# A scan and a two-layer product: the second layer as seven half-block products, and casts and transposing DMAs in strict turns

## The chip, the cores and the metric

One core of one Trainium2 chip. The metric is device time in microseconds (us) of one execution; lower is better. A time is about 2 us longer than the span of the same execution in the trace.

## The reference

```python
# x, f_logit: (4, 6144, 256); lower_bound: (256,); w1, w2: (256, 1024); w_out: (1024, 256)
f = lower_bound + (1 - lower_bound) * sigmoid(f_logit)
h = zeros((B, D))
for t in range(S):                       # a recurrence along the 6144 steps
    h = f[:, t] * h + (1 - f[:, t]) * x[:, t]
    y[:, t] = h
y = y.reshape(24576, 256)
out = np.maximum(y @ w1, y @ w2) @ w_out
```

Both kernels use max(a, b) = a + relu(b - a). So the first layer is `relu(y @ (w2 - w1))`, 1024 wide, and the second layer adds `that @ w_out` to `y @ (w1 @ w_out)`; both kernels fold the factor (1 - lower_bound) into the weights.

## The kernel before

Tokens come in blocks of 512. Two blocks make a chunk of 1024 tokens, which the recurrence needs with features on the partitions. So each chunk of each input is cast from fp32 to bf16 by a DMA from DRAM into a scratch buffer in DRAM (issued on GpSimd, "POOL"), and transposed by a DMA from there into SBUF (issued on the sync engine, "SP"). Chunks 4 to 25, 22 of them, go that way; "cast" and "transpose" below mean these DMAs.

The parts that matter here, abridged:

```python
NSCR = 2                                  # two scratch buffers per tensor
def fetch(c):                             # casts of chunk c
    for s in range(2):                    # f, then x
        scr = scratch[s][uses[s] % NSCR]; uses[s] += 1
        nc.gpsimd.dma_start(out=scr..., in_=src...)
def cross(c):                             # transposes of chunk c
    for s in range(2):
        dst = inpool.tile([P, KC, CH], BF16, name=("fT", "xT")[s])
        nc.sync.dma_start_transpose(out=dst[:, :, 0:nt], in_=held[c, s][0:nt, :])
# ... cut: gate() is a sigmoid on ScalarE; scan_steps() is decay, drive and scan on VectorE
def first_layer(j, fc):                   # 2 matmuls of 512 columns, 1 relu
    ...
def second_layer(j, slot):                # 5 matmuls of 256 columns
    ...   # left = y or relu(..) of 128 tokens (weights of the array), right = w13 or w_out
for j in range(2, NBLK + 1):
    ahead("cross", cross, j + LEAD_CROSS)     # 3 blocks ahead
    ahead("fetch", fetch, j + LEAD_FETCH)     # 7 blocks ahead
    for fc in range(FC):                      # 8 slots
        first_layer(j, fc); second_layer(j - 1, fc)   # + gate, scans of block j + 1
```

A cast waits only until the transpose that read its own scratch buffer has landed.

Of the kernel before, what the change touches and what calls it, by code (L numbers as in the profile page):

```python
# [18 lines left out]
def kernel(  # L19
# [18 lines left out]
    CH = 1024  # L38
    assert S % CH == 0

# [15 lines left out]
    def by_xbar(c, s):  # L56
        return c >= 4
# [6 lines left out]
    natpool = ctx.enter_context(tc.tile_pool(name="nat", bufs=6))  # L64
    inpool = ctx.enter_context(tc.tile_pool(name="inp", bufs=5))
    midpool = ctx.enter_context(tc.tile_pool(name="mid", bufs=2))
    ypool = ctx.enter_context(tc.tile_pool(name="ypool", bufs=4))
    rpool = ctx.enter_context(tc.tile_pool(name="rpool", bufs=2 * FC + 4))
    opool = ctx.enter_context(tc.tile_pool(name="opool", bufs=4))
    ps_t = ctx.enter_context(  # L70
        tc.tile_pool(name="ps_t", bufs=2, space=bass.MemoryType.PSUM)
    )
    ps_d = ctx.enter_context(
        tc.tile_pool(name="ps_d", bufs=3, space=bass.MemoryType.PSUM)
    )
    ps_o = ctx.enter_context(
        tc.tile_pool(name="ps_o", bufs=3, space=bass.MemoryType.PSUM)
    )

    NSCR = 2  # L80
    scratch = [
        [dram.tile([CH, D], BF16, name=f"scr{s}_{q}") for q in range(NSCR)]
        for s in range(2)
    ]
    uses = [0, 0]
# [5 lines left out]
    def fetch(c):  # L91
        b, t0, nt, _ = chunks[c]
        for s in range(2):
            src = srcs[s][b, t0 : t0 + nt, :]
            if by_xbar(c, s):
                scr = scratch[s][uses[s] % NSCR]
                uses[s] += 1
                nc.gpsimd.dma_start(  # L98
                    out=scr[0:nt, :].rearrange("(p i) d -> p (i d)", p=P),
                    in_=src.rearrange("(p i) d -> p (i d)", p=P),  # L100
                )
                held[c, s] = scr
            else:
                nat = natpool.tile([P, CH // P, D], BF16, name=("fn", "xn")[s])
                nc.gpsimd.dma_start(
                    out=nat[:, 0 : nt // P, :].rearrange(
                        "p (k i) d -> p k (i d)", i=TB // P
                    ),
                    in_=src.rearrange(
                        "(k p i) d -> p k (i d)", p=P, i=TB // P  # L110
                    ),
                )
                held[c, s] = nat
# [3 lines left out]
    def fetch_first(k):  # L117
        nt = TB // 2
        for s in range(2):
            raw = const.tile([P, nt // P, D], FP32, name=f"raw{k}{s}")  # L120
            nc.sync.dma_start(  # L121
                out=raw[:],
                in_=srcs[s][0, k * nt : (k + 1) * nt, :].rearrange(
                    "(p i) d -> p i d", p=P
                ),
            )
            raws[k, s] = raw

    def first_bf16(k, s, copy):
        raw = raws[k, s]  # L130
        nat = const.tile([P, raw.shape[1], D], BF16, name=f"nat{k}{s}")
        copy(out=nat[:], in_=raw[:])
        raws[k, s] = nat

    def first_turn(k):
        nt = TB // 2
        for s in range(2):
            dst = ps_t.tile([P, KC, nt // P, P], BF16, name="tT")
# [9 lines left out]
    def cross(c):  # L148
        nt = chunks[c][2]
        for s in range(2):  # L150
            if by_xbar(c, s):
                dst = inpool.tile([P, KC, CH], BF16, name=("fT", "xT")[s])
                nc.sync.dma_start_transpose(  # L153
                    out=dst[:, :, 0:nt], in_=held[c, s][0:nt, :]
                )
                held[c, s] = dst

    def turn_steps(j):
        b, t0, nb, c, o = blocks[j]
        steps = []  # L160
        for s in range(2):
            if by_xbar(c, s):
                turned[j, s] = held[c, s][:, :, o : o + nb]
                continue
            dst = ps_t.tile([P, KC, TB], BF16, name="tT")
            ns = nb // P
            turned[j, s] = dst[:, :, 0:nb].rearrange("p k (i m) -> p k m i", i=ns)
            for q in range(ns):
                for h in range(KC):
                    steps.append(  # L170
                        (
                            dst[:, h, q * P : (q + 1) * P],
                            held[c, s][:, o // P + q, h * P : (h + 1) * P],
                        )
                    )
# [7 lines left out]

    us = {}

    def gate(j):
        nb = blocks[j][2]
        u = midpool.tile([P, KC, TB], BF16, name="u")
        fT = turned[j, 0]
        nc.scalar.activation(  # L190
            out=like(u[:, :, 0:nb], fT), in_=fT, func=AF.Sigmoid, scale=-1.0
        )
        us[j] = u
# [6 lines left out]
    def scan_steps(j):  # L200
        b, t0, nb, c, o = blocks[j]
        u = us[j]
        ff = midpool.tile([P, KC, TB], BF16, name="ff")
        v = midpool.tile([P, KC, TB], BF16, name="v")
        y = ypool.tile([P, KC, TB], BF16, name="y")
        ys[j] = y

        def decay(h):
            nc.vector.tensor_scalar(  # L209
                out=ff[:, h, 0:nb],  # L210
                in0=u[:, h, 0:nb],
                scalar1=nom[:, h : h + 1],
                scalar2=1.0,
                op0=ALU.mult,
                op1=ALU.add,
            )

        def drive():
            xT = turned[j, 1]
            nc.vector.tensor_tensor(  # L220
                out=like(v[:, :, 0:nb], xT),
                in0=like(u[:, :, 0:nb], xT),
                in1=xT,
                op=ALU.mult,
            )

        def scan(h):
            if t0 == 0:
                init = 0.0
            else:  # L230
                pn = blocks[j - 1][2]
                init = ys[j - 1][:, h, pn - 1 : pn]
            nc.vector.tensor_tensor_scan(  # L233
                out=y[:, h, 0:nb],
                data0=ff[:, h, 0:nb],
                data1=v[:, h, 0:nb],
                initial=init,
                op0=ALU.mult,
                op1=ALU.add,
            )  # L240

        return [
            lambda: decay(0),
            lambda: decay(1),
            drive,
            lambda: scan(0),
            lambda: scan(1),
        ]

    first = {}  # L250

    def first_recurrence(k):
        nt = TB // 2
        cols = slice(k * nt, (k + 1) * nt)
        if k == 0:
            for t in ("u", "ff", "v"):
                first[t] = midpool.tile([P, KC, TB], BF16, name=t)
            ys[0] = ypool.tile([P, KC, TB], BF16, name="y")
        u, ff, v, y = (*(first[t] for t in ("u", "ff", "v")), ys[0])
        fT, xT = raws[k, 0], raws[k, 1]  # L260
        nc.scalar.activation(
            out=like(u[:, :, cols], fT), in_=fT, func=AF.Sigmoid, scale=-1.0
        )
        for h in range(KC):
# [7 lines left out]
            )  # L272
        nc.vector.tensor_tensor(
            out=like(v[:, :, cols], xT), in0=like(u[:, :, cols], xT), in1=xT,
            op=ALU.mult,
        )
        for h in range(KC):
# [13 lines left out]

    ident_f = const.tile([P, P], FP32)
# [8 lines left out]
    wdf = wpool.tile([P, KC, DFF], FP32)  # L301
    wd = wpool.tile([P, KC, DFF], BF16)
    w1T = wpool.tile([P, FC, D], BF16)
    w13 = wpool.tile([P, KC, D], BF16)
    NG = 2
    NQ = FC // NG
    w1n = [wpool.tile([P, KC, NQ * P], FP32, name=f"w1n{g}") for g in range(NG)]
    w2n = [wpool.tile([P, KC, NQ * P], FP32, name=f"w2n{g}") for g in range(NG)]

    def half(w, g):  # L310
        return w[g][:].rearrange("p kc (m q) -> p kc q m", q=NQ)

    def fcs(w, kc, g):
        return w[:, kc, g * NQ * P : (g + 1) * NQ * P].rearrange(
            "p (q m) -> p q m", q=NQ
        )
# [12 lines left out]
    def make_wd(fc, n):  # L329
        g, r = divmod(fc, NQ)  # L330
        qs = slice(r, r + n)
        cols = slice(fc * P, (fc + n) * P)
        nc.vector.tensor_tensor(  # L333
            out=wdf[:, :, cols].rearrange("p kc (q m) -> p kc q m", q=n),
# [4 lines left out]
        for kc in range(KC):  # L339
            if g == 0:  # L340
                nc.scalar.mul(wd[:, kc, cols], wdf[:, kc, cols], om[:, kc : kc + 1])  # L341
            else:
                nc.vector.tensor_scalar_mul(
                    out=wd[:, kc, cols], in0=wdf[:, kc, cols], scalar1=om[:, kc : kc + 1]
                )

    def turn_w1(k):
        g, r = divmod(k, NQ // 2)
        pt = ps_o.tile([P, KC, 2, P], FP32, name="psO")
# [11 lines left out]
    def make_w13():  # L361
        for kc in range(KC):
            psw = ps_o.tile([P, 2, D], FP32, name="psO")
# [9 lines left out]

    rts = {}

    def first_layer(j, fc):
        nb = blocks[j][2]
        y = ys[j]
        dT = ps_d.tile([P, TB], FP32, name="dT")
        for kc in range(KC):  # L380
            nc.tensor.matmul(  # L381
                dT[:, 0:nb],
                lhsT=wd[:, kc, fc * P : (fc + 1) * P],
                rhs=y[:, kc, 0:nb],
# [3 lines left out]
        rt = rpool.tile([P, TB], BF16, name="rt")  # L388
        nc.scalar.activation(out=rt[:, 0:nb], in_=dT[:, 0:nb], func=AF.Relu)  # L389
        rts[j, fc] = rt  # L390
# [3 lines left out]
    def second_layer(j, slot):  # L394
        b, t0, nb, c, o = blocks[j]
        ns = nb // P
# [3 lines left out]
        for k in range(slot * total // FC, (slot + 1) * total // FC):  # L400
            i, s = divmod(k, n)
            g, r = divmod(i, 2)
            if s == 0 and (r == 0 or j == NBLK - 1):
                acc["ps"] = ps_o.tile([P, 2, D], FP32, name="psO")
# [3 lines left out]
            left = y[:, s, i:nb:ns] if s < KC else rts[j, s - KC][:, i:nb:ns]  # L408
            right = w13[:, s, :] if s < KC else wob[:, s - KC, :]
# [8 lines left out]
            if j == NBLK - 1 and s == n - 1:  # L418
# [3 lines left out]
                r0 = b * S + t0  # L422
                (nc.sync if r else nc.scalar).dma_start(
# [148 lines left out]
```

## Time and profile before

| kernel before | time, us |
|---|---|
| first three runs | 438.17, 401.23, 438.83 |
| with the run beside the changed kernel | median 419.7, 400.81 to 438.83 |

There are two kinds of runs: fast ones near 401 us and slow ones. The profile that the prediction had is of a slow one, span 428.3 us.

From the page of that profile: busy time by engine, and the chain of work that ended last (shares of the span). PE is TensorE, PEld its weight loads, DVE VectorE, ACT ScalarE, POOL GpSimd, SP the sync engine; a q after a name marks that engine's queue of issues and waits.

```profile
PE 392.8 (92%) x2744; PEld 296.8 (69%) x2792; DVE 248.7 (58%) x359; ACT 268.5 (63%) x447; POOL 26.4 (6%) x58
...
PE 46%; DMA 34%; SPq 15%; ACT 3%; DVE 1%; issue 1%; ACTq 0%
```

TensorE (PE) is busy 92% of the time, yet half of the chain is DMA and the sync queue. The timeline of the sync engine in the same profile (start in us, duration in us, what) shows why:

```profile
200.80 7.09 SPq L153 DMA_TRANSPOSE fT<-scr_0_90  x1
207.99 5.61 SPq L153 DMA_TRANSPOSE xT<-scr_0_92  x1
213.69 1.03 SPq L433 DMA_DIRECT2D out_dram<-osb  x2
214.82 9.81 SPq L153 DMA_TRANSPOSE fT<-scr_1_91  x1
224.73 9.85 SPq L153 DMA_TRANSPOSE xT<-scr_1_93  x1
234.67 1.01 SPq L433 DMA_DIRECT2D out_dram<-osb  x2
235.78 10.23 SPq L153 DMA_TRANSPOSE fT<-scr_0_90  x1
```

One chunk took 14.0 us (200.8 to 214.8), the next 21.0. The timeline of TensorE, one slot in steady state, gives the other pace:

```profile
204.67 0.59 PE L381 MATMUL dT<-y,wd 128*128 128x512 bf16 x2
205.10 0.71 PE L410 MATMUL psO<-wob,rt 128*128 128x256 bf16 x5
205.65 0.59 PE L381 MATMUL dT<-y,wd 128*128 128x512 bf16 x2
```

From 204.67 to 205.65 is 0.98 us a slot, with 16 slots a pair of blocks (a slot is 2 first-layer matmuls and the second-layer ones that go with them). TensorE needs 15.64 us a pair (the exact figure is from the trace, as the time from one pair's first weight load of the first layer to the next pair's).

### The profile page before, as it was taken

Reading aid. Unit: us, or ns where it says so; the run is one execution under the profiler, and the core shown is the slowest. Engines: PE = TensorE matmul, PEld = TensorE weight load, DVE = VectorE, ACT = ScalarE, POOL = GpSimd, SP = SyncE. Lnnn points to the kernel's source line nnn. Section 1 sums busy time; section 2 is a strip of 40 time slices with the busy share of each in tenths; the row PEclk is TensorE's granted clock in tenths of the full one; section 3 lists DMA queues with packets and bytes.
Section 4 is the critical chain, followed back from the end, with each engine's and each line's share of the span. In section 5 each row is a group of like instructions: output and inputs, shape, how many; then the busy total and the mean of one; then the engine's idle time right before and its main releaser. Section 6 shows DMA issues by size and latency. Waiting matters only on the chain.

```text
span 428.3 us, 6970 instructions
## 1 busy us (share of the span) xinstructions
PE 392.8 (92%) x2744; PEld 296.8 (69%) x2792; DVE 248.7 (58%) x359; ACT 268.5 (63%) x447; POOL 26.4 (6%) x58
## 2 busy tenths in 40 slices
PE   3999979798789999998997899999998999999996
PEld 1677756576557777776775577767676777777775
DVE  5785637455357566564653557657547656567551
ACT  3656656557366676675673666756657676776762
POOL 1400000000000000000000000000000000000000
PEclk9999999999989999999999699999999999999999
DMA  7999999999999999999998999999999999998112
GB/s 245 222 220 198 123 157 141 137 169 252 81 240 226 119 239 233 112 248 168 183 237 75 218 158 186 250 145 170 219 131 231 226 216 164 268 157 179 79 69 100
DMA packets 103377, 77.01 MB, mean 180 GB/s; under 512 B 93552, under 2 KB 94064, under 8 KB 102640
## 3 DMA queue, kind: packets, MB, share of 16 engines
q1 hardware_dynamic: 100512, 51.13, 66.7%
q0 software_dynamic: 2544, 25.17, 36.1%
q8 instruction: 22, 0.36, 0.4%
q10 hardware_dynamic: 288, 0.26, 0.2%
q14 instruction: 11, 0.09, 0.1%
HBM read 53.48 MB, written 48.23 MB: 237 GB/s over the span
## 4 chain that ended last, share of the span: by engine, by line
PE 46%; DMA 34%; SPq 15%; ACT 3%; DVE 1%; issue 1%; ACTq 0%
PE psO L410 25%; DMA fT<-scr_0_90 20%; PE dT L381 19%; SPq L153 13%; DMA fT<-scr_1_91 12%; ACT u L190 2%; DMA w1n_110<-in_moe_w_dram 2%; SPq L433 1%; PE psO L352 1%; ACT rt L389 1%; PE tT L180 1%; PE psO L365 0%; SPq L121 0%; DVE osb L430 0%; DVE y L233 0%
## 5 line engine op out<-in xcount | busy, mean ns | idle before, releaser
L389 ACT ACTIVATE rt<-dT 128x512 bf16<-128x512 f32 x384 | 219.2, 598 | 104.1 <-PE dT L381 100.0
L381 PE MATMUL dT<-y,wd 128*128 128x512 bf16 x720 | 219.5, 384 | 21.3 <-ACT rt L389 19.5
L410 PE MATMUL psO<-wob,rt 128*128 128x256 bf16 x1536 | 230.7, 274 | 2.7 <-issue 0.4
L410 PEld LDWEIGHTS <-rt 128*128 128x128 bf16 x1536 | 170.7, 114 | 41.4 <-issue 1.1
L233 DVE TENSOR_TENSOR_SCAN y<-ff,y,v 128x512 bf16<-128x512 bf16 x88 | 107.9, 1268 | 0.1
L430 DVE COPY osb<-psO 128x512 f32<-128x512 f32 x94 | 64.7, 690 | 59.0 <-PE psO L410 58.9
L381 PEld LDWEIGHTS <-wd 128*128 128x128 bf16 x768 | 75.8, 99 | 33.2 <-issue 24.6
L209 DVE TENSOR_SCALAR ff<-u,nom 128x512 bf16<-128x512 bf16 x94 | 29.0, 351 | 105.0 <-ACT u L190 105.0
L410 PE MATMUL psO<-w_109,y 128*128 128x256 bf16 x384 | 74.0, 275 | 0.0
L410 PEld LDWEIGHTS <-y 128*128 128x128 bf16 x384 | 43.4, 113 | 42.6 <-issue 3.5
L190 ACT ACTIVATE u<-fT 128x1024 bf16<-128x1024 bf16 x44 | 46.4, 1054 | 35.5 <-DMA fT<-scr_1_91 18.2
L220 DVE TENSOR_TENSOR v<-u,xT 128x1024 bf16<-128x1024 bf16 x44 | 30.3, 688 | 3.8 <-DMA xT<-scr_0_92 1.8
L98 POOL DMA_DIRECT2D scr_0_90<-in_f_logit_dram x11 | 5.4, 493 | 149.7 <-DMA fT<-scr_0_90 149.7
L98 POOL DMA_DIRECT2D scr_1_91<-in_f_logit_dram x11 | 5.3, 486 | 148.8 <-DMA fT<-scr_1_91 148.1
L233 DVE TENSOR_TENSOR_SCAN y<-ff,v 128x512 bf16<-128x512 bf16 x6 | 7.0, 1208 | 0.0
L98 POOL DMA_DIRECT2D scr_0_92<-in_x_dram x11 | 5.4, 488 | 18.7 <-DMA xT<-scr_0_92 16.9
L98 POOL DMA_DIRECT2D scr_1_93<-in_x_dram x11 | 5.3, 486 | 15.7 <-DMA xT<-scr_1_93 14.9
L190 ACT ACTIVATE u<-tT 128x1024 bf16<-128x1024 bf16 x3 | 3.2, 1058 | 4.3 <-PE tT L180 4.3
L352 PE MATMUL psO<-ident_f,w1n_110 128*128 128x128 f32 x8 | 1.9, 422 | 3.4 <-DMA w1n_110<-in_moe_w_dram 3.4
L341 ACT ACTIVATE wd<-wdf,om 128x128 bf16<-128x128 f32 (+1 forms) x6 | 2.2, 428 | 4.3 <-DVE wdf L333 4.3
L352 PEld LDWEIGHTS psO<-ident_f,w1n_110 128*128 128x128 f32 x8 | 1.6, 221 | 3.7 <-issue 3.7
L220 DVE TENSOR_TENSOR v<-u,tT 128x1024 bf16<-128x1024 bf16 x3 | 3.6, 1216 | 0.0
(49 smaller groups left out, 45.1 us busy)
## 6 DMA issues: line engine op xcount, KB each, us to landing
out_dram<-osb SPq DMA_DIRECT2D x47, 512.0 KB, 4.8
scr_0_90<-in_f_logit_dram POOLq DMA_DIRECT2D x11, 512.0 KB, 7.5
scr_0_92<-in_x_dram POOLq DMA_DIRECT2D x11, 512.0 KB, 12.4
scr_1_91<-in_f_logit_dram POOLq DMA_DIRECT2D x11, 512.0 KB, 7.9
scr_1_93<-in_x_dram POOLq DMA_DIRECT2D x11, 512.0 KB, 13.6
fn<-in_f_logit_dram POOLq DMA_DIRECT2D x3, 256.0 KB, 7.9
xn<-in_x_dram POOLq DMA_DIRECT2D x3, 256.0 KB, 8.6
w2n_112<-in_moe_w_dram SPq DMA_DIRECT2D x1, 512.0 KB, 6.5
```

The source lines that it names most:

```text
L98: nc.gpsimd.dma_start(out=scr[0:nt, :].rearrange("(p i) d -> p (i d)", p=P), in_=src.rearrange("(p i) d -> p (i d)", p=P),)
L153: nc.sync.dma_start_transpose(out=dst[:, :, 0:nt], in_=held[c, s][0:nt, :])
L180: nc.tensor.transpose(dst, src, ident[:])
L190: nc.scalar.activation(out=like(u[:, :, 0:nb], fT), in_=fT, func=AF.Sigmoid, scale=-1.0)
L209: nc.vector.tensor_scalar(out=ff[:, h, 0:nb], in0=u[:, h, 0:nb], scalar1=nom[:, h : h + 1], scalar2=1.0, op0=ALU.mult, op1=ALU.add,)
L220: nc.vector.tensor_tensor(out=like(v[:, :, 0:nb], xT), in0=like(u[:, :, 0:nb], xT), in1=xT, op=ALU.mult,)
L233: nc.vector.tensor_tensor_scan(out=y[:, h, 0:nb], data0=ff[:, h, 0:nb], data1=v[:, h, 0:nb], initial=init, op0=ALU.mult, op1=ALU.add,)
L352: nc.tensor.transpose(pt[:, kc, q, :], half(w1n, g)[:, kc, 2 * r + q], ident_f[:])
L381: nc.tensor.matmul(dT[:, 0:nb], lhsT=wd[:, kc, fc * P : (fc + 1) * P], rhs=y[:, kc, 0:nb], start=(kc == 0), stop=(kc == KC - 1),)
L389: nc.scalar.activation(out=rt[:, 0:nb], in_=dT[:, 0:nb], func=AF.Relu)
L410: nc.tensor.matmul(ps[:, r, :], lhsT=left, rhs=right, start=(s == 0 and (r == 0 or j == NBLK - 1)), stop=(s == n - 1 and (r == 1 or j == N ...
L430: nc.vector.tensor_copy(out=osb[:, 2 * g : 2 * g + 2, :], in_=ps[:])
```

## The change

Two things at once. First, the second layer is computed over pairs of blocks: the four quarters of the pair's relu output and of w_out are combined as in Winograd's form of Strassen's product, with seven products of half blocks instead of eight. That takes four sums on VectorE and intermediate copies, and matmuls of 128 columns. Second, to stop the 401/438 scatter, there is one scratch per tensor. Both transposes of a chunk must land before the next two casts start, and those must land before the next transposes start.

```diff
     def cross(c):
-        for s in range(2):
-            if by_xbar(c, s):
-                dst = inpool.tile([P, KC, CH], BF16, name=("fT", "xT")[s])
-                nc.sync.dma_start_transpose(out=dst[:, :, 0:nt], in_=held[c, s][0:nt, :])
-                held[c, s] = dst
+        for s in (1, 0):
+            dst = inpool.tile([P, KC, CH], BF16, name=("fT", "xT")[s])
+            nc.sync.dma_start_transpose(out=dst[:], in_=scratch[s][:])
+            held[c, s] = dst
+        if c + 1 < NCHUNK:
+            for s in (1, 0):
+                pool_waits(held[c, s][:, 0, 0:1])     # a one-column copy on POOL
+            for s in range(2):
+                fetch(c + 1, s)
 ... (cut: buffers; the relu covers two feature blocks and writes its tokens reordered)
+    def sum3(p):      # and sum2, sum1, sum4: [128 x 2048] bf16 on VectorE
+        sum_of(p, 3, quarter(p, 0, 0), quarter(p, 1, 0), ALU.subtract)
+    def sevenths(p):
+        product("X", part(0, 0), lambda k: wob[:, k, lo], True)
+        then(snapshot("X", 1))                        # ScalarE copy out of PSUM
+        product("B", part(0, 1), lambda k: wob[:, KH + k, lo], True)
+        linear("B", ja, lo, False)
+        then(leave("B", ja, lo, 1, False))            # VectorE addition out of PSUM
+        product("X", sub(2), lambda k: t2[:, k, :])
 ... (cut: four more products, three more linear parts)
+        for p in range(PAIR0, NPAIR):
+            for slot in range(2 * FC):
+                first_layer(2 * p + slot // FC, slot % FC)
+                ...   # 9 steps of sevenths(p - 1); sums of p - 1; scans of p + 1
+                if slot == 2 and p + 3 < NPAIR: cross(chunk of pair p + 3)
+                if slot in gates: pair_gate(p + 2, gates[slot])
```

The changed kernel works as a pipeline of pairs: in turn p it runs the first layer of pair p, the second layer of p - 1, the scans of p + 1, the gates of p + 2 and the transposes of p + 3.

## The prediction

> **What bounds it now.** In steady state (timeline, 200-215 us) one slot takes 0.98 us: 2 first-layer matmuls (0.43) and 5 second-layer ones (0.55). That is 7.8 us a block, 15.6 a pair; 47 blocks of it after the first 27.4 us make about 398 us, so the 401 us run is TensorE-bound. The profiled run (428.3) and the 438 us runs lose the rest to DMA: the page has PE at 92%, but the chain of waits has 34% DMA (fT transposes) and 15% sync-queue issue. Transposing DMAs are issued every 17.0 us on average from 26.9 to 383.6 us (sync queue timeline), against 15.6 of matmul work. One cycle differs from another: 14.0 us at 200.8, 21.0 at 214.8; in the DMA packet records the slow ones have casts and transposes in flight together for 12-13 us where 6 suffices elsewhere.
>
> **What the change does to TensorE.** A pair's second layer was 80 matmuls of 256 columns (8.74 us). Now it is 7x16 product plus 32 linear matmuls of 128 columns: 144. Back-to-back 128-column bf16 matmuls, each with its own weight load, are in this trace: 16 block transposes in 0.89 us (chain, 21.26 us), 56 ns each. The Trainium skill, "TensorE: Matmul & The Clock Gate", section "Back-to-back issue gap", says about 81 ns for such pairs; this trace disagrees, so I use 56. Second layer 8.06 + first layer 6.88 = 14.95 us a pair, 0.7 less; times 21 pairs, 14 us. At 81 ns it would be 18.5 and a loss.
>
> **Other engines, per pair (estimates from durations).** VectorE: decay 0.9, drive 1.4, scans 4x1.22=4.9, four sums of 2048 columns about 1.2 each=4.9, three additions out of PSUM 0.7 each=2.1: 14.2 us, from 10.3. ScalarE: 8 double-width relus about 1.03, four gates 0.6, four copies 0.6: 13. So VectorE comes within 1 us of TensorE; some of the 0.7 is lost in waits for sums or for banks.
>
> **DMA.** Strict turns: two transposes, then two casts, nothing overlapping. Cast packets take 2.43 us each: two 5.3 with spread. Two transposes 4-5 of packets. Launch latencies, now exposed twice: pool wait 0.3, cast issue to first packet 2.1-3.9, transpose issue to packet 2-3.2, plus landings. Sum 15 to 18 us a pair, less erratic. Below 15 TensorE bounds; at 16 DMA still does. The skill, "DMA: Bandwidth & Descriptors", section "Issuing engines are not separate DMA queues", says all queues share 16 engines; the trace agrees (a transpose waits out the cast packets ahead of it). So the gain over 438 is mostly steadiness (up to 37 us), and the seven products are worth at most 14 us over the 401 state.
>
> **Prediction: 402 us**, range 385 to 440. Faster by over 2%: 0.74; within 2%: 0.12; slower: 0.14. TensorE-bound throughout would be about 388; turns of 16 us give about 420.
>
> **What would show it.** Second-layer matmuls 144 a pair at 56 ns pace, slot time about 0.93 us; PE busy share above 92%; VectorE share about 80-90%; POOL's wait for fT and xT once a pair; no transpose overlapping a cast; issue-to-landing of transposes down from 16 to under 9 us; the chain of waits mostly PE, little DMA. All runs close together rather than 401/438.
>
> **What would make it wrong.** (a) Strict turns take 17-18 us: then every pair waits for fT, PE share falls under 85% and the time is 450 or more. (b) Weight loads do not hide behind 128-column matmuls (strided y loads): pair over 16 us. (c) VectorE in order: a sum or a PSUM addition late behind scans stalls TensorE. (d) TensorE stalls drop its granted clock to half, as at 120-140 us in the profile before.

## The result, and the profile after

| | runs, us | median |
|---|---|---|
| before, same chip | 438.17, 401.23, 438.83, 400.81 | 419.7 |
| changed | 428.66, 434.13, 434.96 (fast), 438.63 (slow) | 434.54 |

The ratio of fast runs is 1.0786, 95% interval 1.068 to 1.089: slower. (A ratio is the mean time of one kernel's fast runs over that of the other's in the same rounds, so it is not quite the ratio of the medians quoted.) The predicted 402 us and the range 385 to 440 were for a gain; 434.54 lies inside the range, but there was no gain. Below, the changed kernel's profile (span 426.6, fast) is compared with the slow one of before and, where it matters, with a profile of before in its fast state (span 399.8, taken as e11 below).

From the page of the changed kernel, the same parts as before:

```profile
PE 381.8 (90%) x4064; PEld 283.0 (66%) x4136; DVE 322.9 (76%) x383; ACT 288.8 (68%) x383; POOL 50.8 (12%) x100
...
DMA 64%; PE 16%; SPq 11%; POOL 5%; issue 2%; ACT 2%; DVE 0%; POOLq 0%; ACTq 0%
```

The chain is now mostly DMA: casts (36% of the span) and transposes (25%), with the sync queue's issue and POOL's between them. Here is one link of that chain in order of time (start, us, what): a turn.

```profile
246.00 8.36 DMA scr<-in_x_dram
254.36 0.02 SPq L145
...
254.41 2.06 SPq L145
...
256.57 4.29 DMA fT<-scr
...
260.99 0.72 POOL waited L332
261.71 0.42 POOL scr L94
262.13 7.96 DMA scr<-in_x_dram
```

x's cast lands, two transposes are issued and land, POOL's copy sees it, the next casts are issued: nothing of it overlaps. From 246.00 to 262.13 the turn took 16.1 us. The sync engine's timeline has transposes first issued at 27.92 and last at 368.08 us: 340.16 / 21 = 16.2 us a chunk on average. Without the start, between 90 and 375 us, it is 16.35 us; every turn below is measured in this window, from one issue of x's transpose to the next.

Nothing else paces this loop: in all 22 chunks x's transpose is issued within 0.07 us of the landing of x's cast. TensorE is not part of it. (Its granted clock was at half in five stretches, 24 us together, each beginning in or within 1 us after an idle time of TensorE of 2.6 to 4.8 us; the mean is 0.972, against 0.998 in the fast profile of before. So point (d) of the prediction did happen, but it does not lengthen the turn.)

The matmuls themselves ran as predicted. Timeline of TensorE, unstalled:

```profile
255.52 0.59 PE L419 MATMUL dT<-y,wd 128*128 128x512 bf16 x2
255.95 0.67 PE L597 MATMUL ps<-wob,r 128*128 128x128 bf16 x9
256.45 0.59 PE L419 MATMUL dT<-y,wd 128*128 128x512 bf16 x2
```

0.93 us a slot, nine 128-column matmuls in 0.50 us. Unstalled pairs took 14.95 us to the hundredth.

So the first reading, theory A: the turn of about 16.2 us binds, the engines could do 14.95, and the gain of the products lies off the chain. The rival, B: the seven-product form needs over 16 us on the engines (VectorE at 76%), and the DMA only adapts to it.

### The profile page after: what moved, and what is told of

It is laid out like the page before. It is cut to its first block, busy times and chain, and to the rows that moved or that the text cites. A ratio compares the mean times of both kernels' runs of the same rounds, so it can differ in the third digit from the quotient of the medians.

```text
span 426.6 us, 9503 instructions
## 1 busy us (share of the span) xinstructions
PE 381.8 (90%) x4064; PEld 283.0 (66%) x4136; DVE 322.9 (76%) x383; ACT 288.8 (68%) x383; POOL 50.8 (12%) x100
## 4 chain that ended last, share of the span: by engine, by line
DMA 64%; PE 16%; SPq 11%; POOL 5%; issue 2%; ACT 2%; DVE 0%; POOLq 0%; ACTq 0%
DMA scr<-in_x_dram 36%; DMA fT<-scr 25%; SPq L145 10%; PE dT L419 7%; PE ps L597 5%; PE ps L466 4%; POOL waited L332 3%; POOL scr L94 2%; DMA wob<-in_moe_w_out_dram 1%; DMA r<-in_moe_w_dram 1%; ACT r L427 1%; ACT u L268 1%; SPq L112 0%; ACT sn L543 0%; SPq L612 0%
## 5 line engine op out<-in xcount | busy, mean ns | idle before, releaser
L427 ACT ACTIVATE r<-dT 128x1024 bf16<-128x1024 f32 x192 | 196.3, 1025 | 72.7 <-PE dT L419 72.5
L597 PEld LDWEIGHTS <-S 128*128 128x128 bf16 x1344 | 91.5, 100 | 59.5 <-issue 27.4
L597 PE MATMUL ps<-t,S 128*128 128x128 bf16 x1008 | 79.3, 223 | 22.5 <-ACT sn L543 22.2
L597 PEld LDWEIGHTS <-r 128*128 128x128 bf16 x1008 | 66.9, 98 | 27.2
L268 ACT ACTIVATE u<-fT 128x512 bf16<-128x512 bf16 x88 | 55.0, 628 | 42.0 <-DMA fT<-scr 41.9
L555 DVE TENSOR_TENSOR osb<-ps,sn 128x512 f32<-128x512 f32 x63 | 43.2, 686 | 36.4 <-PE ps L597 30.4
L488 DVE TENSOR_TENSOR S<-r 128x2048 bf16<-128x2048 bf16 x42 | 51.1, 1218 | 4.0 <-ACT r L427 4.0
L597 PE MATMUL ps<-wob,r 128*128 128x128 bf16 x672 | 51.2, 219 | 0.5
L488 DVE TENSOR_TENSOR S<-r,S 128x2048 bf16<-128x2048 bf16 x42 | 50.9, 1211 | 0.9 <-ACT r L427 0.9
L597 PE MATMUL ps<-w,y 128*128 128x128 bf16 x504 | 49.5, 221 | 0.4
L466 PEld LDWEIGHTS <-r 128*128 128x128 bf16 x192 | 19.4, 101 | 4.6 <-issue 0.6
```

What stands on the lines that cost most here:

```text
L268: nc.scalar.activation(out=mids[p + NBLK, "u"][:, h, cols], in_=held[c, 0][:, h, cols], func=AF.Sigmoid, scale=-1.0,)
L427: nc.scalar.activation(out=rts[j, k][:, g - 1 : g + 1, :].rearrange("p q (i m) -> p q i m", m=P), in_=dT[:].rearrange("p q (m i) -> p q i ...
L466: nc.tensor.matmul(ps[:, r, :], lhsT=left, rhs=right, start=(s == 0 and (r == 0 or j == NBLK - 1)), stop=(s == n - 1 and (r == 1 or j == N ...
L488: nc.vector.tensor_tensor(out=t[:], in0=a, in1=b, op=op)
L555: nc.vector.tensor_tensor(out=dst, in0=bank[b][:], in1=snap[name][:], op=ALU.add)
L597: nc.tensor.matmul(bank[b][:, i, :], lhsT=a, rhs=w, start=fresh, stop=after is not None, skip_group_check=True,)
```

## The experiments

The turn is read from the DMA packet records and the POOL and SP timelines; the pair times are read as said above. The diffs are condensed: lines are joined or left out. The runs were taken on several chips, each beside runs of the kernel before on the same chip, so times of two experiments are best compared by their ratios to before.

### e1: the changed kernel's compute alone

```diff
+        if c >= 7:                       # chunks 7.. read chunk 6 again: wrong on purpose
+            for s in range(2): held[c, s] = held[6, s]
+            return
```

> The changed kernel with its compute kept, but casts and transposes stop after chunk 6; later pairs read that chunk again (result wrong on purpose), so no DMA but the output stores is left in the steady state. Theory A (turn-bound: the pair period of 16.2 us is the DMA turn; the engines could do 14.9): 385 to 395 us, pairs at 14.9 to 15.2 us. Rival B (engine-bound: sums, snapshots and 128-column matmuls themselves need over 16 us a pair and the DMA only fits itself to them): stays at 420 to 435 us.

399.33 us median (398.81 to 399.84, four runs), ratio to before 0.9951. From the fourth pair on, every pair takes 14.94 to 14.95 us, after 15.11 for the first of them. B falls: with no cast or transpose in the way the engines hold 14.95. In the window from 100 to 370 us VectorE is busy 240 of 270 us and still stalls nothing. The waits that the profile lists between 90 and 360 us (who waits for whom, us in total, times, longest) are these, and none is TensorE's:

```profile
ACT r L433 <- PE dT L425: 54.0, 109, 0.8
DVE ff L202 <- ACT u L274: 27.7, 18, 1.5
DVE osb L561 <- PE ps L603: 0.5, 3, 0.2
```

But the expected total of 385 to 395 was missed, because the start was slower: the third pair begins at 54.5 us and the fourth at 71.1, against 47.1 and 62.7 in the fast profile of before.

### e2: the compute of before alone

The same cut in the kernel before.

> The kernel before with the same cut (no casts or transposes after chunk 6, wrong result on purpose). Both theories: 398 to 402 us, the TensorE pace of 15.6 us a pair. The difference to the run of the changed kernel with the same cut is what the seven products are worth when nothing else binds: A says 8 to 14 us less for the changed kernel, B says the changed kernel is slower than this.

401.31 us (400.90 to 401.53), pairs of 15.64 us. So the 401 state of before is its matmul pace, and without DMA the change is worth 2 us, not 14. The difference is in the start (below).

### e3: the changed compute with the DMA order of before

```diff
-    scratch = [dram.tile([CH, D], BF16, name=f"scr{s}") for s in range(2)]
+    scratch = [[dram.tile([CH, D], BF16, name=f"scr{s}_{q}") for q in range(2)] for s in range(2)]
-        for s in (1, 0):
+        for s in range(2):
-        if c + 1 < NCHUNK:
-            for s in (1, 0): pool_waits(held[c, s][:, 0, 0:1])
-            for s in range(2): fetch(c + 1, s)
+        if c + 2 < NCHUNK:
+            for s in range(2): fetch(c + 2, s)
```

> The changed kernel's compute with the DMA order of before: two scratch buffers per tensor, f before x, a cast waits only for the transpose that frees its own buffer, no turns. A: the period falls under 16.2 us; good runs near 388 to 395 us, perhaps scattered up to 430 as the kernel before is. B: 425 to 435 us as the changed kernel.

427.02, 437.06, 445.38 and 452.33 us (the first is the profiled one). Its pairs average 16.6 us ((397.2 - 65.1) / 20) and range from 14.95 to 22.6. This was a miss for A as I had put it. The strict turns alone are not what costs: without them the same compute is no faster and scatters more. With this compute, fed one chunk at a time, the DMA needs over 16 us in either order.

### e4: the kernel before with the strict turns alone

```diff
-    NSCR = 2
+    NSCR = 1
-        for s in range(2):
+        for s in (1, 0):
+        if c >= 4 and c + 1 < NCHUNK:
+            for s in (1, 0): pool_waits(held[c, s][:, 0, 0:1])
+            fetch(c + 1)
-    LEAD_CROSS = 3
+    LEAD_CROSS = 6
-            ahead("fetch", fetch, j + LEAD_FETCH)
```

> The kernel before with only the strict turns added: one scratch per tensor, x then f transposed, both awaited on POOL, then the next casts; transposes issued up to 6 blocks ahead. A: the turn binds here too, 16.2 to 16.5 us a chunk, 412 to 425 us in every run, no 401 state. B: 400 to 404 us, since TensorE needs 15.6 anyway and the turns would cost nothing.

402.43 us (401.63 to 402.98, four runs), ratio 1.0031. This was again a miss for A in its number, and it corrects the theory. The turn is 15.68 us here (mean of 17 turns) and follows itself without a pause (x's transpose within 0.06 us of the landing of its cast, in all 22 chunks), yet TensorE needs 15.64 a pair, so little is lost: the pairs average 15.79 us, with four of the twenty from the fourth on longer than 15.64. Its chain of waits:

```profile
PE 47%; DMA 40%; SPq 6%; DVE 2%; issue 2%; POOL 2%; POOLq 0%; DVEq 0%
```

Half TensorE, half DMA: two limits within 0.04 us of each other. That is theory A2: **in strict turns the DMA has no slack. Making TensorE faster than 15.6 us a pair exposes a feed that takes 15.7 to 16.4.** It is shown for the turns only; how fast the feed of before could run in its own order, with the old compute, no run measured (see e11). The turns by themselves do what they were for: these four runs lie within 0.4% of each other, while the eight runs of before beside them go from 400.6 to 434.7.

### e5: the turn without POOL's copies

```diff
-            for s in (1, 0):
-                pool_waits(held[c, s][:, 0, 0:1])
```

(The casts still wait through their scratch.)

> The changed kernel without the two GpSimd copies that await the transposes; the casts still wait for them through their own scratch, and f's cast waits for the last transpose, so the order of the turn is kept. The copy in front of the casts takes 0.18 to 1.68 us in the changed kernel. Theory A2 (the turn, at 16.35 us against a matmul pace of 14.95, sets the steady state, so whatever shortens the turn shortens the run by 20 times that): turn 16.35 to about 15.9, 416 to 423 us. Rival (something else holds the pairs at 16.4 and the turn follows): unchanged, 428 to 436.

425.0 us (420.08 to 426.26), pairs 16.2 on average instead of 16.4. The ratio to before is 1.058 (1.047 to 1.069), against 1.0786 (1.068 to 1.089) of the changed kernel. The time lies in neither expected range, and the turn fell to 16.20 us, not to 15.9. By the packet records and POOL's timeline the step from the last transpose packet to the next cast's issue fell from 1.38 to 1.17 us, so the copies cost about 0.2 us a turn; as a gain of the whole run this is hardly clear of noise (e6 comes as low). POOL's timeline in the changed kernel (start, duration, what, idle before):

```profile
129.76 1.68 POOL L332 CAST waited<-fT 128x1 f32<-128x1 bf16 x1 [1.28 <-DMA fT<-scr]
...
260.99 0.72 POOL L332 CAST waited<-fT 128x1 f32<-128x1 bf16 x1 [1.83 <-DMA fT<-scr]
```

and in e4:

```profile
160.64 0.29 POOL L331 CAST waited<-fT 128x1 f32<-128x1 bf16 x1 [1.69 <-DMA fT<-scr]
```

One column, 0.18 us when nothing is in the way, up to 1.68. The Trainium skill, "GPSIMD Engine Reference", section "Key points", says that GpSimd shares its SBUF interfaces with VectorE and contends with VectorE instructions that have two SBUF inputs or run in a two-port mode. The trace agrees: of the 42 copies of the changed kernel 28 take over 0.25 us, and each of these ends within 0.05 us of the end of a VectorE operation. The average copy takes 0.60 us there (VectorE busy 76%, many operations of two inputs) and 0.26 us in e4 (62%).

### e6: the changed kernel without the four sums

```diff
-        t = spool.tile([P, HC, TB], BF16, name="S")
-        nc.vector.tensor_tensor(out=t[:], in0=a, in1=b, op=op)
-        sums[p, name] = t
+        sums[p, name] = a                # wrong result on purpose
```

> The changed kernel with the four VectorE sums of a pair left out; the products read the unsummed tiles (wrong result on purpose), matmuls and DMA as they are. Why is the turn 16.35 us here and 15.68 with the old compute? Theory V (VectorE's traffic to SBUF slows transposes and POOL): turn near 15.7, about 410 to 416 us. Rival S (VectorE has nothing to do with it; the stores, now two together, or chance): turn stays 16.2 to 16.4, 425 to 435 us.

426.67 us (424.57 to 431.2), ratio to before 1.063 (1.054 to 1.073); turn 16.28 us against 16.35. Theory V falls for the sums: 102 us of VectorE's work, they are not what lengthens the turn to 16.35. Its other work is not excluded: the average copy on POOL still takes 0.50 us here. The ratio is nearly that of e5, so neither run's small gain should be read closely.

### e7: turns of two chunks

```diff
+        if c >= NCHUNK or c % 2: return
+        for k in (c, c + 1):
             for s in (1, 0):
-                nc.sync.dma_start_transpose(out=dst[:], in_=scratch[s][:])
+                nc.sync.dma_start_transpose(out=dst[:], in_=scratch[s][k % 2][:])
...     # then all four waited for, then the casts of c + 2 and c + 3
```

> The changed kernel with turns of two chunks: four transposes, then four casts, two scratch buffers per tensor. The hand-over times (about 4.5 us a turn: launches, landings, the copy) are then paid once in two pairs: estimate (4x2.6 + 4x2.9 + 4.5)/2 = 13.3 us a pair, below TensorE's 14.95, and chunk 5 is there early, so most of the 12.9 us that the start loses is gone too. A2: 386 to 394 us, pairs of 14.95 us, faster than both kernels. If something other than the turn held it: 420 or more.

397.33 us (396.14 to 401.35), correct, ratio 0.993 (0.984 to 1.002), so not clear of before. Every pair from the fifth on takes 14.95 us, and the chain of waits is TensorE's:

```profile
PE 87%; DMA 1%; ACT 1%; SPq 0%; DVE 0%; issue 0%; ACTq 0%
```

With the same casts and transposes as the changed kernel, but half as many hand-overs, the feed is out of the way. The steady state is as A2 says. The total missed the expected 386 to 394, again by the start: the second and third pair took 18.2 and 14.4 us.

### e8: stores issued from ScalarE's queue

```diff
-        (queue or nc.sync).dma_start(
+        (queue or nc.scalar).dma_start(
```

> The changed kernel with the output stores issued from the scalar engine's queue, not behind the transposes in the sync queue. If the stores in the transposes' own queue lengthen the turn (theory S): transposes' packets go from 5.3 to 4.6 us, turn 15.7, 412 to 420 us. If not: turn unchanged, 426 to 438 us (ScalarE pays about 1 us a pair for issuing, which it has).

463.8 us (460.92 to 466.95), worse than either expectation. The turn is 18.20 us and the pairs average 18.05; the transposes' packets take 6.77 us instead of 5.29. In the sync queue the stores stand behind the transposes and mostly run in the gap while the casts are being launched: by the packet records between 90 and 375 us, 329 of 4357 store packets start among transpose packets. From ScalarE's queue it is 1326 of 4096. This undoes theory S, and it confirms A2 from the other side: with a turn 1.85 us longer the pairs are 1.65 us longer and the span goes from 426.6 to 462.1 us.

### e9: two-chunk turns with later gates at the start

```diff
-            for s in (1, 0):             # f is transposed before x
+            for s in (0, 1):
-            if fc % 2: pair_gate(PAIR0, fc // 2)          # among second_layer(1)
+            if fc in (1, 3):                              # among second_layer(2), half a pair later
+                pair_gate(PAIR0, fc - 1); pair_gate(PAIR0, fc)
+            if first: gates = {12: 0, 13: 1, 14: 2, 15: 3}
+                if first and slot in (1, 3, 5, 7): pair_gate(p + 1, slot // 2)
...     # and the scans that need them correspondingly later
```

> The two-chunk turns with a later start-up: the gates of the first three pairs (ScalarE, in order with the relus) stand where their chunk has landed instead of up to 10 us earlier, f is transposed before x. In the two-chunk run the pairs 2 and 3 took 18.2 and 14.4 us where their matmuls need 11.5 and 11.3: 9.8 us lost, with ScalarE waiting 10.5 us for fT. Theory H (those gates, waiting at the head of ScalarE's queue, hold up the relus and so TensorE): 3 to 8 us less than 397, that is 389 to 394 us, steady pairs still 14.95. If the start is lost for another reason (VectorE, weights): 396 to 399 us.

392.78 us (391.9 to 393.43, six runs), correct, ratio 0.980 (0.9786 to 0.9815): theory H holds for nearly half of the 9.8 us, and this version beats both kernels (before by 2.0%), with no slow run among six. The run also transposes f before x, so it doesn't tell the later gates from the earlier f. ScalarE's timeline shows the start, first the changed kernel:

```profile
34.45 2.19 ACT L268 ACTIVATE u<-fT 128x512 bf16<-128x512 bf16 x4 [2.54 <-DMA fT<-scr]
...
41.38 1.02 ACT L427 ACTIVATE r<-dT 128x1024 bf16<-128x1024 f32 x1 [0.74 <-PE dT L419]
48.98 0.63 ACT L268 ACTIVATE u<-fT 128x512 bf16<-128x512 bf16 x1 [6.57 <-DMA fT<-scr]
49.51 1.01 ACT L427 ACTIVATE r<-dT 128x1024 bf16<-128x1024 f32 x1
```

and e9:

```profile
41.00 1.02 ACT L434 ACTIVATE r<-dT 128x1024 bf16<-128x1024 f32 x1 [0.74 <-PE dT L426]
41.92 1.14 ACT L273 ACTIVATE u<-fT 128x512 bf16<-128x512 bf16 x2
42.96 1.02 ACT L434 ACTIVATE r<-dT 128x1024 bf16<-128x1024 f32 x1
```

In the changed kernel a gate stands in ScalarE's queue before its chunk has landed, and the relus behind it wait, although their matmuls are done (6.57 us at one of them). The Trainium skill, "TensorE: Matmul & The Clock Gate", section "Architectural detail: the array is 16× 32×32, not 1× 128×128", says ScalarE's queue is strictly first in, first out; this trace agrees. In e9 the relus come first. Its fourth and fifth pairs still took 17.4 and 16.4 us, so some 4 us of the start are still to be had.

### e10: half of the product matmuls left out

```diff
-                for k in range(n):
+                for k in (0, n - 1):     # wrong result on purpose
```

> The changed kernel with half of each product's matmuls left out (k = 0 and 3 only; wrong result on purpose): 56 of 144 second-layer matmuls a pair less, so about 150 KB less of instructions are fetched and TensorE needs about 12 us a pair. Theory A2 (the turn sets the pace whatever TensorE needs): still about 16 us a pair, 415 to 428 us, though a quarter of the matmul work is gone. Theory F (fetches of instructions, 16 KB each, lengthen the transposes that they meet; 32 fetches here, 22 with the old compute): fetches fall to about 23 and the turn from 16.35 to about 16.0. If the matmuls set the pace instead: pairs of 12 us, below 360 us.

420.61 us (414.29 to 421.98), ratio of fast runs 1.041 (1.031 to 1.051) against 1.079, pairs 16.0 us on average, TensorE busy 80%. This is the plainest evidence that the turn, and not TensorE, sets the pace: with 56 of 144 second-layer matmuls of each pair gone, the run is only 3% faster, and DMA still leads its chain of waits:

```profile
DMA 56%; PE 14%; SPq 8%; POOL 5%; DVE 3%; issue 2%; ACT 1%; POOLq 0%; ACTq 0%
```

The page's line for the queue that fetches instructions, of the changed kernel and of this one (packets, MB, share):

```profile
q8 instruction: 32, 0.52, 0.5%
```

```profile
q8 instruction: 23, 0.38, 0.4%
```

Each fetch is one packet of 16 KB. In the changed kernel the packets of x's transpose take 2.24 us on average where no fetch falls into them and 2.71 where one does; of f's, 2.47 and 3.30. With nine fetches fewer, the turn fell from 16.35 to 16.08 us (its profile is of a run with a TensorE clock of 0.947; the turn is a DMA time), and the fall is in the transposes' packets (5.3 to 5.0 us a turn). That is the size which theory F expected. But the run changed more than the fetches, and the turns of e5 and e6 (16.20 and 16.28 us) also differ from 16.35 with all 32 fetches, so it is supported rather than settled.

### e11: the kernel before again

> The kernel before, unchanged, for a profile in its fast state (the profile at hand spans 428.3 us, while most runs take 401). Expected: span about 399 us, pairs of 15.64 us from first to last, no wait of ScalarE for fT after the start; if it falls in the other state again, it shows pairs of 15.64 mixed with ones of 17 to 22 us.

401.61 and 434.93 us; the profile fell in the fast state (span 399.8). All pairs from the third on take 15.64 us, with no wait of ScalarE for fT after the start; the chain of waits is

```profile
PE 96%; DMA 2%; issue 1%; SPq 1%; DVE 0%
```

This is the profile to compare with. It says that TensorE binds; it does not say how near the turns bring the DMA. That took e4. In its own order the feed was not at a limit here: from the sixth chunk on, f's cast lands 14 to 19 us before its transpose is issued, and the sync queue spends 190 us waiting for finished outputs that it has to store.

## Why the prediction was wrong, point by point

The difference of the spans, 426.6 - 399.8 = 26.8 us (changed against before, both fast), by the times at which pairs begin:

| stretch | before | changed | difference |
|---|---|---|---|
| to the fourth pair | 62.7 | 70.8 | +8.1 |
| 20 pairs to the last | 312.8 | 328.1 | +15.3 |
| last pair and rest | 24.3 | 27.7 | +3.4 |

Twenty pairs at the matmul pace would have been 20 x (15.64 - 14.95) = 13.8 us shorter; they are 15.3 longer, so the feed takes back 29.1 us. (The turn alone gives 20 x (16.35 - 14.95) = 28 us.) In the start the changed kernel even has one block's second layer (4.4 us) less to do, which it does at the end instead, so about 12.5 us are stalls there. Products -14, feed +29, start +12.5 give the 27 us.

1. **Right: the matmul pace.** "Second layer 8.06 + first layer 6.88 = 14.95 us a pair, 0.7 less; times 21 pairs, 14 us": measured 14.95 against 15.64. The 56 ns from the transposes held for the products.
2. **Right: the other engines.** VectorE comes close to TensorE's pace and binds nowhere (e1, e6).
3. **Wrong, and decisive: the path.** The step that failed is the choice of TensorE as what binds ("the chain of waits mostly PE, little DMA"): the turn binds, at 16.35 us against 14.95. The prediction's own sum allowed it: "Sum 15 to 18 us a pair … Below 15 TensorE bounds; at 16 DMA still does." The sum was right as a range, 16.35 us measured, and the sentence after it named the consequence; but 402 us, between its own 388 (TensorE alone) and 420 (turns of 16 us), needs a turn of about 15.4 (an estimate by interpolation). The mis-sized terms were the packets: two casts 6.34 us against 5.3, two transposes 5.29 against "4-5"; launches were shorter than feared (1.31 and 1.39 us), and landings with the copy came to 2.0. Case (a) under what would make it wrong is what happened, at 16.35 instead of 17 to 18 us: TensorE's busy share stayed at 90%, so that share, which I had named as the sign (under 85%), would have misled. That 434.54 lies inside the stated range is owed to the width of the range, not to the argument.
4. **Wrong: "TensorE-bound throughout would be about 388".** Without DMA it is 399 (e1). The start was not costed at all: gates two pairs ahead, in ScalarE's queue ahead of the relus, wait for chunks that the turns deliver 14.5 us apart.
5. **Wrong: the base.** "the gain over 438 is mostly steadiness": against the slow state the change is worth 1%, and against the fast state it loses 7.9%. The turns do bring steadiness (e4), but the products raise the demand above what the turns can feed.
6. **Half right: "no transpose overlapping a cast; issue-to-landing of transposes down from 16 to under 9 us".** No packet of one overlaps the other in the steady turns, and f's transpose lands 4.3 us after its issue in the chain above. "the chain of waits mostly PE, little DMA" was the opposite.

Still open: why the turn is 16.35 us with the new compute and 15.68 with the old. Of the 0.67 us, 0.50 lie in the transposes' packets (5.29 against 4.79 us a turn) and 0.16 in the hand-over from them to the next casts (1.38 against 1.22). More instruction fetches among the transposes and slower POOL copies fit these two, but no run isolates them, and e6 excludes only VectorE's sums. Why before has a slow state also stays open beyond this: between 90 and 360 us casts and transposes have packets in flight together for some 98 us in its slow profile and for none in its fast one (e11), and with turns (e4) no slow run was seen in four.

## What to carry to other kernels

Before you speed up the engine that binds, find out how far off the next limit is: here a run with the matmuls unchanged and the feed serialized, as the change would have it (e4), showed it at a distance of 0.04 us a pair, which no busy share had shown. If a serial chain of hand-overs becomes the limit, make each turn carry more (two chunks: 397 us instead of 434) before you shorten its parts. In a queue that runs in order, put an instruction that waits for a DMA where the data will have landed, not as early as the program allows: with f transposed first, that was worth another 5 us.

## What the Trainium skill lacked or had wrong

- "TensorE: Matmul & The Clock Gate", section "Back-to-back issue gap", gives about 81 ns for a sustained pair of weight load and 128-column matmul. Here it is 56 ns: 16 in 0.89 us before the change, and 144 of them with 32 of 512 columns in 14.95 us after it.
- "DMA: Bandwidth & Descriptors", section "Issuing engines are not separate DMA queues", says that DMAs of all issuing engines interleave and that another issuing engine only saves issue time; it does not say that the interleaving can cost. Here it cost 29 us in the median: stores moved to ScalarE's queue ran among the transposes and stretched their packets from 5.29 to 6.77 us a turn (e8).
- No page that I found says that transposes which an instruction fetch (one packet of 16 KB) meets are longer: 2.71 against 2.24 us and 3.30 against 2.47 us here.
